# Chunked attention and a GELU MLP on one core: the first tile's q loads move to ScalarE's queue

## The chip, the cores and the metric

The kernel runs on one core of one Trainium2 chip. The metric is the device time of one execution in microseconds. The kernel before takes 276.42 us, the median of 3 runs (276.33 to 276.53).

## What is computed

Inputs q, k and v have the shape (8, 8, 576, 64): batch, heads, sequence, head size. The sequence is cut into 9 chunks of 64, and attention stays within a chunk. Its result is then laid out as 4608 tokens of 512 values and goes through two matrix products with an exact GELU between them:

```python
scores = scale * q_c @ k_c.T          # per batch, head and chunk of 64
attn   = softmax(scores)              # over the 64 keys of the chunk
x      = (attn @ v_c)                 # -> 4608 tokens x 512
h      = x @ w_in                     # 512 -> 2048
g      = 0.5 * h * (1 + erf(h / sqrt(2)))
out    = g @ w_out                    # 2048 -> 512
```

All inputs and the output are float32 in memory. The kernel casts them to bf16 for TensorE.

## The kernel before

**Tiles.** The 4608 tokens are worked in 9 tiles of 512. Tiles 0 to 7 are the first eight chunks of one batch each; tile 8 gathers the ninth chunk of all batches. A tile's attention is worked in four groups g of two heads. Each tile then has a first MLP product (16 slots of 4 matmuls, line 451; the very first two slots of tile 0 in line 441), a GELU on ScalarE (lines 444 and 453), and a second product.

**Order.** The whole program is written out by hand (`manual_schedule`): every engine executes its instructions in the order of the source. Only semaphores tie the engines together.

**The start (tile 0).** SP issues all loads. First come q and k of tile 0, in four pairs of 256 KB loads, one pair for each group g, in the order q0, k0, q1, k1, q2, k2, q3, k3 (line 118, called from lines 701 to 703). Then come the eight loads of V, 128 KB each in rows of 256 bytes (line 157), and the weights of the first product (line 676). The loads take turns on eight completion semaphores, so each load from the ninth on first waits for the load eight places ahead of it to complete: the first V load waits for q0, the second for k0, and so on.

The arriving float32 data is cast to bf16 (line 164): q on VectorE, k on GpSimd, which also zeroes the block-diagonal k tiles `k_bd` (lines 76 and 77) and later casts V (line 169). For each group there are five steps, and the prediction uses their names:

- `T[2g]`: TensorE transposes q of the group (line 175, four matmuls), and VectorE copies the result out (line 181).
- `T[2g+1]`: TensorE transposes k, and ScalarE copies it into `k_bd` in two halves (line 188).
- `S_[g]`: eight matmuls make the scores (line 332), and ScalarE takes the exponential (line 334, tile `pT`).
- `U[0]`, `U[1]` and `att_sum_pe` for groups 2 and 3: the sums for the softmax (lines 340 to 349, 383 to 397; the last in float32 matmuls, line 393).
- `A[g]`: eight matmuls with V (line 406), and VectorE multiplies by the reciprocal sums into `x` (line 408).

TensorE's order at the start is: seven `keep_warm` matmuls on a zero tile (line 693), `T[0]`, `T[1]`, three warm ones, `T[2]`, `S_[0]`, `T[3]`, one warm, `T[4]`, one warm, `S_[1]`, `U[0]`, `T[5]`, `T[6]`, `T[7]`, `U[1]`, `S_[2]`, one warm, `S_[3]`, one warm, then the sums of groups 2 and 3 and `A[0]` to `A[3]`. The first product follows directly.

**ScalarE at the start.** Its first instruction is the load of the table for the exponential, with one small activation on `act_scratch` (lines 706 and 698). Then it copies `k_bd` of group 0, takes the exponential of group 0, copies `k_bd` of group 1, takes the exponential of group 1, copies `k_bd` of groups 2 and 3, and takes the last two exponentials. After these comes the table for GELU.

**Weights.** Four quarters of `w_in` and four of `w_out` arrive as float32 in a pool of six staging buffers shared with q, k and V, and are cast by VectorE, GpSimd and ScalarE (lines 679 and 687) while TensorE already works on tile 0's first product.

Of the kernel before, what the change touches and what calls it, by code (L numbers as in the profile page):

```python
# [11 lines left out]
def kernel(  # L12
# [9 lines left out]
    nc = tc.nc  # L22
# [8 lines left out]
    J = 4  # L31
# [6 lines left out]
    MT = CT * CH  # L38
# [60 lines left out]
    def stage_tile():  # L99
        return stage.tile([P, SW], f32, tag="stage", name="arrival")  # L100
# [5 lines left out]
    def load_qk(t, nm, h0=0, h1=H):  # L106

        st = tiles[t]
        src = q if nm == "q" else k
        if nm + "f" not in st:  # L110
            st[nm + "f"] = stage_tile()[:].rearrange("p (h j d) -> p h j d", h=H, j=J)
            st[nm] = ld.tile([P, G, J, 2, D], bf16, tag=nm, name=f"{nm}_nat")
        raw = st[nm + "f"]
        if t == K0 and nm == "k":
            for n in range(CT // 2):
                nc.sync.dma_start(raw[:, :, n], src[t, :, P * n:P * (n + 1), :].rearrange("h key d -> key h d"))
        elif t < B:
            nc.sync.dma_start(raw[:, h0:h1], src[t, h0:h1, 0:MT, :].rearrange("h (p j) d -> p h j d", j=J))
        else:
            for b in range(B):  # L120
                nc.sync.dma_start(
                    raw[PC * b:PC * (b + 1), h0:h1],
                    src[b, h0:h1, MT:S, :].rearrange("h (p j) d -> p h j d", j=J))
# [576 lines left out]
    with tc.manual_schedule():  # L700
        for g in range(G):
            for nm in "qk":
                load_qk(0, nm, 2 * g, 2 * g + 2)
# [55 lines left out]
        win[0](2, DV)  # L759
        win[0](3, PO)  # L760
        load_qk(1, "q")
        wout.append(load_w_out(1))
        for c in range(1, NWC):
            for i in range(4):
                win[c](i, DV if i % 2 == 0 else PO)
            if c == 1:
                load_qk(1, "k")
            else:
                wout.append(load_w_out(c))
            if c < 3:  # L770
                r = slice(CH * (c - 1), CH * c)
                o = slice(CH * (2 - c), CH * (3 - c))
                nc.gpsimd.memset(v_bds[1][r, :, :, o], 0.0)
# [153 lines left out]
```

## Time and profile before

The profiled execution took 277.47 us. Its span, from the first to the last recorded instruction, is 275.68 us.

| | us | share of the span |
|---|---|---|
| TensorE matmuls busy | 265.6 | 96% |
| TensorE weight loads busy | 170.3 | 62% |
| ScalarE busy | 187.1 | 68% |
| VectorE busy | 177.2 | 64% |
| GpSimd busy | 85.3 | 31% |
| first matmul of the first MLP product starts | 18.98 | |
| median of 3 runs without the profiler | 276.42 | |

In the profile's lines PE is TensorE's matmul, PEld its weight load, DVE is VectorE, ACT is ScalarE, POOL is GpSimd and SP is the engine that issues DMAs; SPq and ACTq are the issuing sides of the queues. A line of the timeline begins with start and length in microseconds, then engine, source line, operation, and the tile written and the tile read. What stands in square brackets is how long the engine idled just before, and what ended it. A line of the busy windows gives a stretch, its length, the busy time and count of PE, PEld, DVE, ACT and POOL, the granted clock of TensorE (1.00 is full), the share of time that the DMA engines were busy, and the GB/s that they moved. A line of the DMA issues gives the tile and the source, the number of issues, their size and the time from the start of the issue until all of it has landed.

### The profile page before, as it was taken

How to read it: one execution, taken by the hardware profiler on the slowest of the kernel's cores; microseconds unless marked ns; L12 is line 12 of the kernel's file. 1: busy time of each engine (PE TensorE's matmuls, PEld its weight loads, DVE VectorE, ACT ScalarE, POOL GpSimd, SP SyncE). 2: the span in 40 equal slices, each digit the busy share in tenths (PEclk: the TensorE clock that was granted, in tenths of full speed). 3: DMA queues.
4: the chain of work that ended last, by engine and by line, in shares of the span. 5: the costliest groups of instructions: out<-in, count | busy, mean ns of one | idle time of the engine just before them, and what ended most of it. 6: DMA issues, size and time to landing. Idle time of an engine off the chain costs nothing.

```text
span 275.7 us, 6639 instructions
## 1 busy us (share of the span) xinstructions
PE 265.6 (96%) x2676; PEld 170.3 (62%) x2697; DVE 177.2 (64%) x321; ACT 187.1 (68%) x350; POOL 85.3 (31%) x142
## 2 busy tenths in 40 slices
PE   6699999999999999999999999999999999999993
PEld 2474455546864686468745874587458745874683
DVE  6866347886743865487998698559955985521521
ACT  3857758888756876687867966796679667346610
POOL 7869768310481354018106600034101100000000
PEclk9979999999999999999999999999999999999998
DMA  6999999798999899999399319999954110130014
GB/s 218 283 342 403 394 386 236 186 247 241 356 303 229 249 292 177 302 306 242 102 249 337 81 56 255 125 128 179 239 134 117 54 64 2 38 117 0 0 40 114
DMA packets 104735, 53.92 MB, mean 196 GB/s; under 512 B 72960, under 2 KB 101632, under 8 KB 104704
## 3 DMA queue, kind: packets, MB, share of 16 engines
q1 hardware_dynamic: 104400, 53.23, 74.6%
q8 instruction: 21, 0.34, 0.5%
q10 hardware_dynamic: 304, 0.26, 0.3%
q14 instruction: 10, 0.08, 0.1%
HBM read 36.70 MB, written 9.44 MB: 167 GB/s over the span
## 4 chain that ended last, share of the span: by engine, by line
PE 91%; ACT 4%; DMA 2%; issue 1%; SPq 0%; ACTq 0%; DVE 0%; POOL 0%; POOLq 0%
PE h_ps L451 43%; PE y_ps L566 34%; PE y_ps L638 3%; PE h_ps L441 2%; DMA arrival<-in_k_dram 2%; PE av_ps L315 2%; ACT k_bd L188 2%; PE s_ps L237 1%; PE y_ps L602 1%; PE rc_ps L393 1%; PE av_ps L406 1%; PE tp L175 1%; ACT pT L244 1%; ACT pT L334 1%; PE s_ps L332 1%
## 5 line engine op out<-in xcount | busy, mean ns | idle before, releaser
L451 PE MATMUL h_ps<-x,w_in_sb 128*128 128x512 bf16 x532 | 118.2, 379 | 0.8
L453 ACT ACTIVATE h<-h_ps 128x512 bf16<-128x512 f32 x137 | 81.7, 598 | 35.5 <-PE h_ps L451 35.5
L451 PEld LDWEIGHTS <-w_in_sb 128*128 128x128 bf16 x548 | 53.6, 98 | 63.2 <-DVE w_in_sb L679 0.2
L164 POOL CAST q_nat<-arrival 128x512 bf16<-128x512 f32 x31 | 20.2, 692 | 66.9 <-DMA arrival<-in_q_dram 66.9
L566 PEld LDWEIGHTS <-h 128*128 128x128 bf16 x384 | 37.0, 98 | 4.7
L566 PE MATMUL y_ps<-v_bd,k_bd 128*128 128x256 bf16 x256 | 29.4, 273 | 0.1
L566 PE MATMUL y_ps<-w_out_sb,h 128*128 128x256 bf16 x256 | 29.3, 273 | 0.0
L212 POOL CAST v_nat<-arrival 128x1024 bf16<-128x1024 f32 x14 | 15.0, 1078 | 45.4 <-DMA arrival<-in_v_dram 45.4
L566 PEld LDWEIGHTS <-k_bd 128*128 128x128 bf16 x256 | 24.8, 98 | 3.2 <-issue 0.2
L533 DVE TENSOR_TENSOR kept<-y_ps,kept 128x512 f32<-128x512 f32 (+1 forms) x25 | 16.4, 657 | 14.6 <-PE y_ps L566 11.8
L698 ACT ACT_TABLE_LOAD x18 | 23.1, 1283 | 1.1 <-PEq L911 0.7
L528 ACT COPY kept<-y_ps 128x512 f32<-128x512 f32 (+1 forms) x26 | 14.5, 556 | 12.4 <-PE y_ps L566 12.2
L164 POOL CAST k_nat<-arrival 128x512 bf16<-128x512 f32 x30 | 18.8, 664 | 10.7 <-DMA arrival<-in_v_dram 6.3
L491 DVE TENSOR_TENSOR s_sb<-h 128x2048 bf16<-128x2048 bf16 x8 | 9.8, 1220 | 18.1 <-ACT h L453 18.1
L504 DVE TENSOR_TENSOR k_bd<-h 128x1024 bf16<-128x1024 bf16 x16 | 11.3, 708 | 14.9 <-ACT h L453 14.9
L566 PE MATMUL y_ps<-v_bd,s_sb 128*128 128x256 bf16 x128 | 15.3, 273 | 0.0
L566 PE MATMUL y_ps<-w_out_sb,s 128*128 128x256 bf16 x128 | 15.3, 273 | 0.0
L566 PE MATMUL y_ps<-v_bd,h 128*128 128x256 bf16 x128 | 15.3, 272 | 0.0
L244 ACT ACTIVATE pT<-s_ps 128x512 bf16<-128x512 f32 x28 | 14.4, 603 | 0.1
L566 PEld LDWEIGHTS <-s 128*128 128x128 bf16 x128 | 12.4, 98 | 1.5
L566 PEld LDWEIGHTS <-s_sb 128*128 128x128 bf16 x128 | 12.3, 98 | 1.5
L538 ACT COPY y_sb<-y_ps 128x512 f32<-128x512 f32 x7 | 4.1, 586 | 13.2 <-PE y_ps L566 13.2
(106 smaller groups left out, 318.2 us busy)
## 6 DMA issues: line engine op xcount, KB each, us to landing
arrival<-in_v_dram SPq DMA_DIRECT2D x58, 128.0 KB, 4.1
arrival<-in_q_dram SPq DMA_DIRECT2D x7, 1024.0 KB, 7.0
arrival<-in_k_dram SPq DMA_DIRECT2D x6, 1024.0 KB, 8.5
out_dram<-kept SPq DMA_DIRECT2D x21, 256.0 KB, 2.6
arrival<-in_moe_w_out_dram SPq DMA_DIRECT2D x4, 1024.0 KB, 12.0
arrival<-in_moe_w_in_dram SPq DMA_DIRECT2D x6, 512.0 KB, 6.2
out_dram<-y_sb SPq DMA_DIRECT2D x11, 256.0 KB, 2.5
arrival<-in_k_dram SPq DMA_DIRECT2D x8, 256.0 KB, 5.5
```

The costliest lines, as they stand in the source:

```text
L164: copy(st[nm][:, g].rearrange("p j r d -> p r j d"), st[nm + "f"][:, 2 * g:2 * g + 2])
L212: copy(st["v"][:, r::2], st["vf"][:, r::2])
L244: nc.scalar.activation(pT[:].rearrange("p u (c j) -> p u c j", j=J), s_ps[g2][c][:].rearrange("p u (j c) -> p u c j", j=J), Act.Exp, scale ...
L451: nc.tensor.matmul(h_ps[:], w_in_sb[:, ks, f * P:(f + 1) * P], tiles[t]["x"][:, ks, :], start=(ks == 0), stop=(ks == KS - 1))
L453: nc.scalar.activation(tiles[t]["h"][:, f, :], h_ps[:], Act.Gelu)
L491: nc.vector.tensor_tensor(s3_sb[:], g_block(t, 0, 0), g_block(t, 1, 0), op=SUB)
L504: nc.vector.tensor_tensor(st["S", i][part], a, b, op=op)
L528: nc.scalar.copy(kept[name][:, ms], ps[:])
L533: nc.vector.tensor_tensor(y_sb[:, ms], ps[:], y_sb[:, ms], op=ADD)
L566: nc.tensor.matmul(to, left(f, m), right[:, f], start=(fresh and (split or m == 0) and f == 0), stop=(f == HF - 1), skip_group_check=True)
L638: nc.tensor.matmul(tiles[t]["y_ps", ms][:], tiles[t]["h"][:, fi, ms * P:(ms + 1) * P], w_out_sb[:, fi, :], start=(fi == 0), stop=False)
L698: nc.scalar.activation(act_scratch[:], rest[:, 0:1], func)
```

## The change

In `load_qk` the engine that issues the load is chosen: for tile 0's q it is ScalarE (`nc.scalar`), and for everything else SP (`nc.sync`) as before. This concerns four loads of 256 KB. In ScalarE's order they stand ahead of the table load; in SP's order k0 to k3 follow each other directly. The data, the buffers, the semaphores that each cast waits for and the order of all other instructions are the same. Line numbers after line 117 are higher by one in the changed kernel.

```diff
         elif t < B:
-            nc.sync.dma_start(raw[:, h0:h1], src[t, h0:h1, 0:MT, :].rearrange("h (p j) d -> p h j d", j=J))
+            by = nc.scalar if t == 0 and nm == "q" else nc.sync
+            by.dma_start(raw[:, h0:h1], src[t, h0:h1, 0:MT, :].rearrange("h (p j) d -> p h j d", j=J))
         else:
```

## The prediction

> **What bounds the kernel now.** I read the page's busy shares first, then the chain of waits, then that chain's first 20 us piece by piece, then the start's timeline, DMA issues and busy windows.
>
> ```profile
> PE 265.6 (96%) x2676; PEld 170.3 (62%) x2697; DVE 177.2 (64%) x321; ACT 187.1 (68%) x350; POOL 85.3 (31%) x142
> PE 91%; ACT 4%; DMA 2%; issue 1%; SPq 0%; ACTq 0%; DVE 0%; POOL 0%; POOLq 0%
> ```
>
> PE is busy 96% of the span, and the chain is PE for 91% of it. The rest is nearly all ahead of the first MLP matmul, which the pieces of the chain in order of time (start, length) show:
>
> ```profile
> 0.74 0.45 SPq L118
> 1.25 0.46 SPq L118
> 1.75 0.47 SPq L118
> 2.26 4.79 DMA arrival<-in_k_dram
> 7.17 0.62 POOL k_nat L164
> 7.85 0.41 PE tp L175 x4
> 8.28 0.58 ACT k_bd L188
> ...
> 12.82 1.09 ACT pT L334 x2
> ...
> 18.98 1.67 PE h_ps L441 x7
> ```
>
> Three issues on SP, the second k load (k1), its cast, its transposes, then ScalarE's row of k_bd copies and exps to 13.91, then PE to 18.98 and PE alone to the end. What the end can move is what 18.98 moves. A step later nothing absorbs it: from 19 us PE shows no wait above 0.3 us.
>
> k1 is not the only late load. Beside it stands q1, in the timeline:
>
> ```profile
> 6.40 0.43 DVE L164 CAST q_nat<-arrival 128x512 bf16<-128x512 f32 x1 [0.81 <-DMA arrival<-in_q_dram]
> 6.88 0.40 PE L175 MATMUL tp<-ident,q_nat 128*128 128x128 bf16 x4 [0.44 <-DVE q_nat L164]
> 7.11 0.40 PE L332 MATMUL s_ps<-s_sb,k_bd 128*128 128x64 bf16 x8
> 7.55 0.60 ACT L334 ACTIVATE pT<-s_ps 128x512 bf16<-128x512 f32 x1 [0.54 <-PE s_ps L332]
> 8.28 1.17 ACT L188 COPY k_bd<-tp 64x512 bf16<-64x512 bf16 x2
> ```
>
> S_[0] stands behind T[2] in PE's order, so the first exp waits for q1. That exp ends at 8.15, only 0.13 us before k_bd copy 1 starts at 8.28. So k1 alone, however early, is worth 0.13 us; beyond that q1 must come earlier too.
>
> **The change: issues.** Four issues (445 to 469 ns each) leave SP and go to ACT; order, waits and counts of all else stay. SP's four k issues then run from 0.74 to 2.78 instead of 1.25 to 4.77, so k1 is issued from 1.25 instead of 2.26. ACT issues q from about 0.75 (where its table load starts now) to 2.8. Behind them wait the table load (1.28 us) and the act_scratch activation (0.20): they end near 4.3 instead of 2.24. The next ACT work is the k_bd copy at 5.83, which now idles 3.59 us, so this costs nothing. If ACT's issue took the 0.73 us of the slower of the two ACT issue groups in the tail, all would end at 5.15, still covered; uncovered, it would cost what it passes 5.83 by.
>
> **What the transfers do.** Times to landing, one line for q1 (issued 1.75) and one for k1 (2.26), then DMA in the busy windows (last two figures: share, GB/s):
>
> ```profile
> arrival<-in_q_dram SPq DMA_DIRECT2D x1, 256.0 KB, 4.6
> arrival<-in_k_dram SPq DMA_DIRECT2D x1, 256.0 KB, 4.8
> ...
> 1.50:2.00 0.50, 0.50 (x2) 0.15 (x1) 0.50 (x1) 0.50 (x1) 0.43 (x3) 1.00 0.16 45
> 2.00:2.50 0.50, 0.50 (x3) 0.20 (x2) 0.45 (x3) 0.23 (x2) 0.43 (x3) 1.00 0.73 238
> 2.50:3.50 1.00, 1.00 (x4) 0.41 (x3) 0.84 (x2) 0.00 (x0) 0.94 (x3) 1.00 0.97 328
> 3.50:4.50 1.00, 0.85 (x4) 0.04 (x2) 0.87 (x2) 0.00 (x0) 0.57 (x2) 1.00 0.85 253
> 4.50:5.50 1.00, 0.46 (x6) 0.29 (x7) 0.61 (x1) 0.00 (x0) 0.77 (x2) 1.00 0.93 309
> ```
>
> Issue plus time to landing gives q0 3.43, k0 4.60, q1 6.37, k1 7.05, q2 7.72, k3 9.79. The engines are 85 to 100% busy from 2.5 us on, so k1 waits for bytes ahead of it, not for its issue (done at 2.73). The earlier issue therefore buys only the ramp: from the first packet at about 1.85 to 2.50 some 142 KB moved (22.5 + 119), where 328 GB/s would have moved 213; the missing 71 KB are 0.22 us. I take 0.2 as won; the ends are 0 and 0.22.
>
> No row has q and k in two queues at once. I take it that the engines serve both in turn. Then q and k of a pair land together at the later slot: q0 and k0 at 4.60 - 0.2 = 4.4, q1 and k1 at 7.05 - 0.2 = 6.85. For k1 that is 0.2 earlier; for q1 it is 0.48 later. Bounds for q1: high 7.05 (no ramp won). Low: 1 MB had moved at 5.55 by the windows, 1.5 us before k1 landed, while the first load landed 0.56 after its bytes; without that lag both land at 5.55 - 0.2 + 0.56 = 5.9. I take 6.85: the lag stands in seven of the eight landings.
>
> The Trainium skill, DMA: Bandwidth & Descriptors, section "Issuing engines are not separate DMA queues", says that DMAs of different engines run on the same 16 DMA engines and interleave, and that issuing from several saves only issue time. The trace agrees in that k1's issue ended 4.3 us before it landed. By that rule the gain in transfer time is nil and the sum below would be without the 0.2.
>
> **The sum.** q1 lands 6.85, cast 0.43 from 6.88. Now POOL casts k1 at the same moment; a DVE cast beside POOL work took 0.60 and 0.78 (at 7.92 and 3.62), beside another POOL cast 0.42 (at 9.62). I take 0.43, with 0.60 as the upper end. T[2] at 7.36, S_[0] at 7.59, the exp at 8.03, k_bd copy 1 about 0.5 us after its start (as at 9.95 to 10.45): 8.53. That is 0.25 later than 8.28. k1's branch: cast 6.88 to 7.50, T[3] after S_[0], done by 8.25: not last. With the bounds: 7.05 and 0.60 give +0.62; 5.9 gives T[2] at 6.41, but k_bd copy 0 (which follows k0's cast by 2.27) ends at 6.70, S_[0] at 6.75, k_bd copy 1 at 7.7, or -0.58. I take +0.3.
>
> From there ScalarE carries +0.3 to the end of its exps: 14.2. q2 and q3 also land up to 0.5 later, with T[4] needed before 9.8 (S_[1]) and its q cast starting now at 7.92: covered, with 0.9 us. k2, k3 come 0.2 earlier, so POOL starts V's casts up to 0.2 earlier; they wait for nobody.
>
> V's loads: each of the eight waits for the completion of the load eight places before it in the program's order. SP is free at 2.78, but the third V load waits for q1, at 6.85 instead of issuing at 6.39; against that, SP's own queue is shorter behind it, and the issues of 1.05, 1.24 and 0.96 us there can fall towards 0.51. The first weights land some 0.5 us earlier to 0.5 later. The trace has 1.6 us between the cast of the second w_in quarter (done 20.61) and its first matmul (about 22.2), and 1.5 or more at each later quarter: covered both ways.
>
> PE's stretch from 14.22 to 18.98 starts 0.3 later and passes it on: 18.98 becomes 19.28. Sum: +0.3 on this execution's 277.47 us (span 275.68). The median of the runs shown is 276.42, 1.05 below the profiled execution; the same step on it gives 276.7. From 0.2% (0.55 us) a measurement of this kernel can tell a difference.
>
> **The clock, which decides the rivals.** The granted clock falls to half once, in stretches of 3.41 us:
>
> ```profile
> 4.12:7.54 3.42, 2.26 (x24) 1.17 (x23) 1.63 (x4) 1.16 (x2) 1.95 (x4) 1.00 0.99 324
> 7.54:10.95 3.41, 2.67 (x32) 1.62 (x32) 2.76 (x6) 2.76 (x5) 3.06 (x7) 1.00 1.10 287
> 10.95:14.36 3.41, 1.91 (x37) 1.20 (x37) 3.29 (x8) 3.32 (x7) 3.01 (x8) 1.00 1.04 281
> 14.36:17.78 3.42, 3.42 (x42) 2.91 (x40) 2.38 (x6) 2.00 (x4) 3.07 (x8) 0.50 1.00 323
> ```
>
> After 1.91 us of PE work in a stretch the next ran at half; after 2.26 it did not. The Trainium skill, TensorE: Matmul & The Clock Gate, section "Part 1: The HAM clock gate", says the gate watches a window of 3.4 us that runs free of the kernel's start. By that rule the stretches could lie elsewhere in every execution; the three runs, 0.20 us apart, don't speak for it.
>
> **Rivals.**
> - *Slower: the clock falls one stretch earlier.* With S_[0] at 7.59 its 0.40 us leave 4.12 to 7.54, and 2.26 becomes 1.86, under 1.91. Then 7.54 to 10.95 runs at half. Eight matmuls of 64 columns took 0.61 there (16.72) and 0.41 at full (18.52): +0.2 each for S_[0] and S_[1], and some 0.1 for the transposes behind. +0.8 in all: 277.2. It decides from S_[0] about 0.35 us later. Against it: the half-rate work then counts longer, and the threshold is only bracketed.
> - *Faster: two queues keep the engines fed and the lag goes.* Landing at 5.9 gives -0.6. PE's final stretch then starts at 13.6, 10.95 to 14.36 holds about 2.5 us of PE work, and the half stretch goes too: the two fp32 groups (1.98 and 1.33 us) fall towards 1.0, worth up to 1.2 more, where POOL's V casts end. Together 274.6 to 275.8, middle 275.2. For it: the share of 0.85 at 3.5 to 4.5. Against: the lag is on few engines, which also work off the second queue.
> - *Nothing: q keeps its place.* If q's queue is served ahead of k's, q1 lands near 6.4 and k1 near 6.9; the exp stays, k1's 0.13 us is all: 276.4.
>
> **How the numbers follow.** Forecast (276.7) 0.34, of it 0.10 above 276.97; slower clock (277.2) 0.30; faster (275.2) 0.18; nothing (276.4) 0.18. So faster 0.18, same 0.24 + 0.18 = 0.42, slower 0.40. The range 275.3 to 277.6 leaves out half of the faster case and a part of the slower. The likeliest case's own range is 276.4 to 277.05.
>
> **What will show it.** In the changed profile: q1 and k1 within 0.2 us of each other near 6.85; the first exp near 8.0 and k_bd copy 1 near 8.5; the table load done by 4.3; first MLP matmul near 19.3. Wrong if q1 lands before 6.3, if the half-clock stretch moves or goes, or if ACT idles for a reason other than q1.

## The result and the profile after

The changed kernel is slower. It takes 278.45 us (median of 22 executions, 276.41 to 279.53) where the kernel before takes 276.66 us (22 executions on the same chip, 275.97 to 277.47). Over all executions the ratio is 1.005, with a 95% interval of 1.0033 to 1.0067; the two medians alone give 1.0065. The forecast was 276.7 us with a range up to 277.6, so the time lies outside it. Two executions that took several times as long as all others are left out here and below: one of the kernel before (558 us) and the traced one of E3 (1544 us), so E3 has no trace.

The median hides the form of it. Together with the first experiment below there are 34 executions of the changed kernel, and they fall into two groups with nothing between 277.43 and 278.4:

| group | executions | from, to | median | mean granted clock of the execution |
|---|---|---|---|---|
| lower | 15 | 276.41 to 277.43 | 276.97 | 0.999 or 1.0 in 14, 0.991 in one |
| upper | 19 | 278.4 to 279.94 | 279.01 | 0.993 to 0.998 in all |

The last column does not show what it seems to. The mean counts recorded stretches at half clock only, and the time ahead of the first clock record counts as full. In the two traces of the changed kernel the only recorded half stretch is the end of the span: 0.5 us in the one at 0.999, 1.8 us in the one at 0.997. One more stretch of 3.41 us at half lowers a mean over 277 us by about 0.006 (an estimate from these figures); the trace before, which has one from 14.36 to 17.78 us and 1.9 us at the end, stands at 0.99. In all runs the means lie at 0.990 to 0.994 or from 0.996 on, with none between. So the ten executions of the upper group at 0.993 or 0.994 probably had such a stretch behind the first rise of the clock, and the nine at 0.997 or 0.998 probably had none. No trace of the changed kernel shows the first kind.

The traced execution that came with the result is of the lower group: 276.81 us, span 275.0. Its busy shares are those of before, which says at once that nothing changed in the long run of the kernel:

```profile
PE 265.2 (96%) x2697; PEld 169.2 (62%) x2697; DVE 178.7 (65%) x321; ACT 187.1 (68%) x350; POOL 85.4 (31%) x142
PE 91%; ACT 4%; DMA 1%; DVE 1%; ACTq 0%; issue 0%
```

The start changed. These are the pieces of the chain of waits in order of time (start, length):

```profile
0.75 3.64 DMA arrival<-in_q_dram
4.39 0.02 issue
4.42 1.16 DVE q_nat L165
5.58 0.05 issue
5.62 0.41 PE tp L176 x4
6.03 0.02 issue
6.05 0.69 DVE s_sb L182
6.75 0.70 DVE q_nat L165
7.45 0.05 issue
7.50 0.40 PE tp L176 x4
7.89 0.25 PE s_ps L333 x8
...
17.89 1.73 PE h_ps L442 x8
```

The chain before ran through k1. Now it starts at q0, and VectorE's casts of q carry it to T[2] at 7.50. The issues of k and of q, four each with the median time to landing, and the busy windows show what the loads did:

```profile
arrival<-in_k_dram SPq DMA_DIRECT2D x4, 256.0 KB, 4.1
arrival<-in_q_dram ACTq DMA_DIRECT2D x4, 256.0 KB, 5.3
```

```profile
2.00:2.50 0.50, 0.50 (x3) 0.19 (x2) 0.45 (x3) 0.00 (x0) 0.43 (x3) 1.00 0.65 182
2.50:3.50 1.00, 1.00 (x4) 0.40 (x3) 0.84 (x2) 0.65 (x1) 0.94 (x3) 1.00 0.85 295
3.50:4.50 1.00, 0.86 (x3) 0.00 (x0) 0.18 (x2) 0.83 (x2) 0.85 (x3) 1.00 1.09 382
4.50:5.50 1.00, 0.00 (x0) 0.00 (x0) 1.00 (x1) 0.00 (x0) 0.95 (x3) 1.00 1.09 349
```

In the last two windows the DMA engines moved 382 and 349 GB/s, where before they moved 253 and 309. The trace's landings are k0 4.09, q0 4.39, k1 5.39, q1 5.81 us, where before they were q0 3.43, k0 4.60, q1 6.37, k1 7.05. The last window also has TensorE at 0.00: it did nothing from 4.5 to 5.5 us. The granted clock of 1.00 in these lines is no measurement up to 4.83 us: the trace's first clock record starts there, and without a record the column prints full.

### The profile page after: what moved, and what is told of

Same layout as the page of the kernel before. It is cut to its first block, busy times and chain, and to the rows that moved or that the text cites. A ratio compares the mean times of both kernels' runs of the same rounds, so it can differ in the third digit from the quotient of the medians.

```text
span 275.0 us, 6660 instructions
## 1 busy us (share of the span) xinstructions
PE 265.2 (96%) x2697; PEld 169.2 (62%) x2697; DVE 178.7 (65%) x321; ACT 187.1 (68%) x350; POOL 85.4 (31%) x142
## 4 chain that ended last, share of the span: by engine, by line
PE 91%; ACT 4%; DMA 1%; DVE 1%; ACTq 0%; issue 0%
PE h_ps L452 43%; PE y_ps L567 34%; PE y_ps L639 3%; PE h_ps L442 2%; PE av_ps L316 2%; ACT k_bd L189 2%; PE s_ps L238 1%; DMA arrival<-in_q_dram 1%; PE y_ps L603 1%; PE tp L176 1%; ACT pT L335 1%; PE av_ps L407 1%; PE rc_ps L394 1%; ACT pT L245 1%; DVE q_nat L165 1%; PE s_ps L333 1%
## 5 line engine op out<-in xcount | busy, mean ns | idle before, releaser
L452 PE MATMUL h_ps<-x,w_in_sb 128*128 128x512 bf16 x548 | 119.7, 379 | 0.0
L165 POOL CAST q_nat<-arrival 128x512 bf16<-128x512 f32 x31 | 19.4, 668 | 64.4 <-DMA arrival<-in_q_dram 64.4
```

What stands on the lines that cost most here:

```text
L165: copy(st[nm][:, g].rearrange("p j r d -> p r j d"), st[nm + "f"][:, 2 * g:2 * g + 2])
L452: nc.tensor.matmul(h_ps[:], w_in_sb[:, ks, f * P:(f + 1) * P], tiles[t]["x"][:, ks, :], start=(ks == 0), stop=(ks == KS - 1))
```

## The experiments

Every experiment was timed beside the kernel before on its own chip. The kernel before had medians of 276.99, 276.74 and 276.74 us beside the three groups of experiments.

**E1: the changed kernel again, without an edit**

> The changed kernel once more, unchanged, for more executions with their clocks and a second trace. Clock theory (a longer gap of TensorE before T[0] lets a stretch of 3.41 us fall to half clock in some executions): times in two groups about 2 us apart, 276.4 to 277.4 where the mean clock is 0.999 or more, 278.4 to 279.5 where it is below 0.9985; median near 278. Transfer theory (two queues land q late in some executions): two groups as well, but not sorted by the clock.

Measured: 278.82 us (276.41 to 279.94, 12 executions), ratio 1.0045 (1.0017 to 1.0073). Five executions were in the lower group and seven in the upper, sorted by the mean clock but for one (277.0 us at 0.991). The traced execution was of the upper group, span 277.1. It shows two things. The first is in the timeline of TensorE up to the first scores:

```profile
5.58 0.61 PE L176 MATMUL tp<-ident,q_nat 128*128 128x128 bf16 x4 [1.22 <-DVE q_nat L165]
6.41 1.49 PE L694 MATMUL warm<-rest 128*128 128x512 bf16 x3
8.12 0.63 PE L333 MATMUL s_ps<-s_sb,k_bd 128*128 128x64 bf16 x8
```

Three warm matmuls took 1.49 us, and 0.81 us in the other trace of the same kernel; T[0]'s transposes took 0.61 and 0.40. TensorE is still at half clock here: this trace's first clock record, at full, starts at 9.04 us, the other trace's at 4.83 us. The scores of S_[0] start at 8.12 instead of 7.73, and the first MLP matmul at 18.25 instead of 17.73: 0.52 us.

The second is larger. These are the pieces of the chain from 18.7 us on, and then the timeline of VectorE and of GpSimd at the same place:

```profile
18.74 0.69 DVE x L409
19.43 2.35 DVE w_in_sb L680
21.78 0.05 issue
21.83 2.33 PE h_ps L452 x10
```

```profile
19.35 2.42 DVE L680 CAST w_in_sb<-arrival 128x512 bf16<-128x512 f32 x1
```

```profile
19.14 0.61 POOL L680 CAST w_in_sb<-arrival 128x512 bf16<-128x512 f32 x1 [0.74 <-DMA arrival<-in_moe_w_in_dram]
19.69 1.80 POOL L774 MEMSET v_bd<- 64x2048 bf16 x1
```

VectorE's cast of the third block of the first quarter of w_in took 2.42 us. In the other trace two such casts took 0.75 us together. It ran into GpSimd's zeroing of the second V tile and ended 0.28 us after it. TensorE needed that block and waited 1.68 us:

```profile
21.83 2.55 PE L452 MATMUL h_ps<-x,w_in_sb 128*128 128x512 bf16 x11 [1.68 <-DVE w_in_sb L680]
```

0.52 and 1.68 are 2.2 us; the spans differ by 2.1 us. The landings of q and k are within 0.33 us of those of the other trace, so q does not land late in this execution of the upper group, which speaks against the transfer theory. The weights do differ: the half quarter that GpSimd casts ahead of the zeroing landed at 19.08 us here and at 20.61 in the other trace, where the zeroing began only at 21.48.

**E2: ten warm matmuls ahead of T[0]**

```diff
-        keep_warm(7)
+        keep_warm(10)
```

> The changed kernel with ten instead of seven warm matmuls ahead of T[0], so that TensorE works until about 5.5 us. Loads untouched. Clock theory: the upper group goes or gets rare, median 276.7 to 277.1, that is the +0.3 us of the late q alone. Transfer theory: as the changed kernel, median about 278.4, with executions above 278.4 in more than a third.

Measured: 276.81 us (276.45 to 279.1, 11 executions), ratio 1.0009 (0.9989 to 1.0029). Nine executions lie at 276.45 to 277.47, and two remain in the upper group (278.4 us at a mean clock of 0.999, 279.1 at 0.994). T[0] starts at 5.59 us, where it also starts without the edit (5.58 and 5.62), so it is TensorE's idle time ahead of T[0], and not T[0]'s lateness, that sends most executions there. The two that remain show that it is not the only way.

**E3: the kernel before with q0's cast held back**

```diff
+        nc.vector.memset(v_bds[0][0:CH, :, :, CH:P], 0.0)
         cast_qk(0, "q", 0, DV)
```

> The kernel before, all loads on SP, with one zeroing of V's tile (0.91 us) done twice on VectorE, so that q0's cast and T[0] start some 0.9 us later while every load stays as it was. Clock theory: an upper group 2 us above appears, in a fifth to two thirds of the executions; median 276.9 to 278.6. Transfer theory: no upper group, at most +0.3 us: 276.6 to 277.0.

Measured: median 276.66 us (276.07 to 278.13, 11 executions), ratio 0.9997 (0.9975 to 1.0019). The median lies below what the clock theory allowed and inside what the transfer theory did. Five of eleven executions lie at 277.33 to 278.13, and none at 278.4 or above. The kernel before beside it had eight of 34 above 277.3. This misses the forecast of a group 2 us higher: a late cast of q0 alone, with all loads on SP, doesn't cost that. How late T[0] was and what the clock did, no trace shows.

**E4: q0 stays on SP, only q1 to q3 on ScalarE**

```diff
-            by = nc.scalar if t == 0 and nm == "q" else nc.sync
+            by = nc.scalar if t == 0 and nm == "q" and h0 > 0 else nc.sync
```

> The changed kernel, but q0 stays first on SP; only q1, q2 and q3 are issued from ScalarE. Clock theory: T[0] is back near 4.5 to 4.8 us, so no upper group, and the late q1 costs 0 to 0.4 us: 276.5 to 277.1. Transfer theory: two queues are still at work, so the upper group stays: median above 278.

Measured: 277.25 us (276.48 to 280.2, 12 executions), ratio 1.0017 (0.9995 to 1.004). T[0] is back at 4.53 us, but k0, now behind q0 on SP, lands at 5.30, and S_[0] stays late at 7.76. Ten executions lie at 276.48 to 277.83. Two are at 278.91 and 280.2, both with a mean clock of 0.993 or 0.994. The median is 0.15 above what the clock theory allowed: two queues with T[0] in time don't bring the upper group back in force, but they don't exclude it.

After these four the theory was: the upper group needs a half-clock stretch somewhere in the first 18 us, and then the zeroing on GpSimd, which the early loads have moved forward, falls on the first weight casts. The next group tests the second half.

**E5: the zeroings of the second V tile one weight quarter later**

```diff
-            if c < 3:
-                r = slice(CH * (c - 1), CH * c)
-                o = slice(CH * (2 - c), CH * (3 - c))
+            if c > 1:
+                r = slice(CH * (c - 2), CH * (c - 1))
+                o = slice(CH * (3 - c), CH * (4 - c))
```

> The changed kernel with GpSimd's two zeroings of the second V tile each one weight quarter later (behind the casts of the third and fourth quarter of w_in), so that the first no longer falls on VectorE's first weight cast. Collision theory (the upper group's 2 us are 0.6 to 0.9 from a clock that rises one stretch late, and the rest from the zeroing that holds up that cast): lower group unchanged at 276.4 to 277.4, upper group at 277.3 to 278.2 instead of 278.4 to 279.9, median 276.9 to 277.5. Rival (the clock alone makes the 2 us): upper group stays at 278.4 to 279.9 in about half of the executions.

Measured: 277.29 us (276.48 to 278.4, 12 executions), ratio 1.0026 (1.0011 to 1.0041). The upper group of 278.4 to 279.94 is gone but for one at its lower edge. Five executions have a clock of 0.990 or 0.991 and lie at 277.34 to 278.4; the other seven lie at 276.48 to 277.8. A half-clock stretch is still there in some executions, but it now costs about 1 us (their median is 278.06) and not 2. That the place of the zeroing makes the other half is shown by the times; the collision itself was seen only in E1's trace.

**E6: the same move in the kernel before**

> The same move of the two zeroings in the kernel before. There the zeroing starts at 21.6 us, behind the cast in question, so both theories expect no change: median 276.5 to 277.2.

Measured: 276.5 us (275.88 to 277.87), ratio 0.9996 (0.998 to 1.0012). Nothing moves, as expected. In the trace of the kernel before the zeroing begins at 21.6 us. It holds up a cast there too, at 22.06 us, but one that TensorE doesn't wait for.

**E7: E2 and E5 together, in the changed kernel**

> The changed kernel with the zeroings moved and ten warm matmuls ahead of T[0]. Both causes are taken away: no executions above 278, median 276.5 to 276.9. If a third cause is at work, some executions stay above 278.4.

Measured: 276.58 us (276.37 to 277.84, 11 executions), ratio 1.0001 (0.9985 to 1.0016). With both causes taken away the changed kernel is as fast as the kernel before. No third cause is needed for the loss. E2's interval overlaps with this one, so the times don't tell how much E5's move adds to E2's.

**E8: the zeroing of the third k tile behind the cast of k1**

```diff
-        zero_k(k_bds[2], nc.gpsimd)
         cast_qk(0, "k", 1, PO)
+        zero_k(k_bds[2], nc.gpsimd)
         zero_k(k_bds[3], nc.gpsimd)
```

> The changed kernel with GpSimd's zeroing of the third k tile moved behind the cast of k1, so that it no longer runs beside VectorE's cast of q0. If that zeroing makes the cast slow (1.15 us): cast 0.4 to 0.8 us, T[0] near 5.1 instead of 5.62, S_[0] 0.3 to 0.5 earlier, lower group at 276.0 to 277.0, and the upper group in fewer executions. If the cast is slow because of the k cast beside it: no change in the cast, both groups as in the changed kernel.

Measured: 276.59 us (276.0 to 277.0, 12 executions), ratio 0.9995 (0.9984 to 1.0006). Here are VectorE's cast of q0 and T[0] in the timeline of the changed kernel, and then in that of E8:

```profile
4.42 1.15 DVE L165 CAST q_nat<-arrival 128x512 bf16<-128x512 f32 x1 [0.82 <-DMA arrival<-in_q_dram]
5.62 0.40 PE L176 MATMUL tp<-ident,q_nat 128*128 128x128 bf16 x4 [1.26 <-DVE q_nat L165]
```

```profile
4.44 0.69 DVE L165 CAST q_nat<-arrival 128x512 bf16<-128x512 f32 x1 [0.84 <-DMA arrival<-in_q_dram]
5.19 0.61 PE L176 MATMUL tp<-ident,q_nat 128*128 128x128 bf16 x4 [0.82 <-DVE q_nat L165]
```

With the zeroing out of its way the cast takes 0.69 us instead of 1.15, and T[0] starts 0.43 us sooner. This swap of two lines alone takes the upper group away in 12 of 12 executions. The clock still rises late in this trace (9.49 us), but TensorE then waits for no weight cast: the zeroing of the second V tile begins at 20.95 us, when VectorE's first two weight casts (19.02 to 19.96 us) are done. So a late clock alone doesn't put an execution into the upper group. Why the weights came later here than in E1's trace is not shown. S_[0] did not come earlier here (7.72 against 7.73), because half-clock matmuls took back what the cast gave.

The last group asks whether the early landings can be turned into time. The order of TensorE is changed so that the scores of group 0 no longer stand behind q1.

**E9: the order alone, in the kernel before**

```diff
-        T[0]()
-        cast_qk(0, "q", 1, DV)
-        T[1]()
+        T[1]()
+        T[0]()
+        cast_qk(0, "q", 1, DV)
         keep_warm(3)
-        T[2]()
         S_[0]()
+        T[2]()
         T[3]()
```

> The kernel before with S_[0] ahead of T[2] and T[1] ahead of T[0] in TensorE's order; all loads on SP. There k0's copy ends at 7.0 and k1 lands at 7.05 us, so nothing can start sooner: k_bd copy 1 stays near 8.2, 276.5 to 277.1 (within 0.2% of before). If it is faster by 0.5 us, the order alone and not the two queues makes the gain of the next kernel.

Measured: 277.08 us (276.28 to 278.0), ratio 1.0007 (0.9987 to 1.0028). Nothing is gained. In its trace k1 landed later than in the kernel before, at 7.92 us, and k_bd copy 1 began at 9.15 us, not near 8.2.

**E10: the same order and E8's swap in the changed kernel**

> The changed kernel with the zeroing of the third k tile moved as in the fourth kernel of the last group, and the same order as h0: T[1] before T[0], S_[0] before T[2]. If the two queues bring k0, k1 and q1 early, as the traces say (k1 at 5.4, q1 at 5.8), and only the order kept that from use: first exp at 6.9 to 7.3, k_bd copy 1 at 7.4 to 7.8 instead of 8.28, end 0.4 to 0.8 us sooner: 275.9 to 276.4. If the early landings are worth nothing: 276.5 to 276.8, as with the zeroing alone.

Measured: 276.41 us (276.06 to 277.35), ratio 0.999 (0.9973 to 1.0006). ScalarE in the timeline:

```profile
5.32 1.17 ACT L189 COPY k_bd<-tp 64x512 bf16<-64x512 bf16 x2 [0.98 <-PE tp L176]
6.99 0.60 ACT L335 ACTIVATE pT<-s_ps 128x512 bf16<-128x512 f32 x1 [0.50 <-PE s_ps L333]
7.49 1.17 ACT L189 COPY k_bd<-tp 64x512 bf16<-64x512 bf16 x2
9.56 0.60 ACT L335 ACTIVATE pT<-s_ps 128x512 bf16<-128x512 f32 x1 [0.91 <-PE s_ps L333]
```

The first exp and the second k_bd copy start at 6.99 and 7.49 as forecast, 0.56 and 0.79 us sooner than before. The second exp starts at 9.56, only 0.39 sooner: it now waits 0.91 us for S_[1], which stands behind T[4] and so behind VectorE's copy of T[2] and cast of q2 (7.26 to 8.62). The time lies between the two forecasts, and its interval includes 1.

**E11: E10 and the move of E5**

> The kernel h1 with the second V tile's zeroings moved one weight quarter later as well. If collisions with the first weight casts still occur in some executions of h1, those go: same lower group, no execution above 277.9. Otherwise as h1.

Measured: 276.37 us (275.96 to 278.2), ratio 0.999 (0.9969 to 1.001). As E10, so nothing shows that E10 had collisions left to remove. One execution, at 278.2 us with a clock of 0.991, lies above the 277.9 that was expected.

**E12: E11 with one more warm matmul behind S_[2] and S_[3]**

```diff
         S_[2]()
-        keep_warm(1)
+        keep_warm(2)
         S_[3]()
-        keep_warm(1)
+        keep_warm(2)
```

> The kernel h2 with one more warm matmul each behind S_[2] and S_[3], where TensorE waits. If a half-clock stretch begins after that place in some executions (mean clock 0.990 to 0.994) for want of work, these executions go and the upper edge falls to about 277.2; the median falls by 0 to 0.3. If not: as h2.

Measured: 276.2 us (275.9 to 276.86, 12 executions), ratio 0.9985 (0.9971 to 0.9999). None of the 12 executions has a clock below 0.997. The time is 0.15% below the kernel before and about 0.65% below the changed one (0.9985 over 1.005). Its margin over the kernel before is hardly clear of the interval, and it is the best of four tries on this chip, so the gain is small at most. E11 had one execution below 0.997, so that the two warm matmuls removed half-clock stretches is not shown.

## Why the prediction was wrong

The sign of the likeliest case was right and its size wrong: +0.3 us was forecast, and the ratio makes 0.5%, about 1.4 us. Two terms that the sum put at nothing make the difference. One is q0's later landing, which leaves TensorE idle ahead of T[0]. The other is the earlier GpSimd ("they wait for nobody", "covered both ways"), whose zeroing meets a weight cast on VectorE. In the traced execution of the upper group the late clock cost 0.52 us and the collision 1.68 us. Taken step by step:

- **Issues.** Right. ScalarE issued q from 0.75 to 2.81 us, its table was loaded by 4.13 and the small activation done by 4.34, and no instruction waited for that.
- **Landings.** Wrong, and for the better. Forecast were 4.4 for q0 and k0 and 6.85 for q1 and k1. Measured were 4.39 and 4.09, then 5.81 and 5.39. The step that failed is "the lag stands in seven of the eight landings", by which it was carried over; that the lag is on few engines, no row shows. All three traces with every load on SP (the kernel before, E6 and E9) have q1 at 6.34 to 7.18; all nine with q's four loads on ScalarE's queue have it at 5.76 to 5.91. The rival "two queues keep the engines fed and the lag goes" had the right premise, with 5.9; its gain of 0.6 us and more did not follow, since VectorE came to q1 late.
- **S_[0] and the exp.** Right numbers for a wrong reason. Forecast were 7.59 and 8.03, with k_bd copy 1 at 8.53; measured 7.73, 8.16 and 8.66. It was not q1's landing that made them late. q0's landing, 0.96 us later than before, moved VectorE's cast of it next to GpSimd's cast of k0 and zeroing of the third k tile, where it took 1.15 us. The prediction wrote q0's landing down and never followed it to T[0]. T[0] went from 4.46 to 5.62, and q1's cast waited on VectorE until 6.66 though its data was there at 5.81.
- **The sum in undisturbed executions.** The lower group's median of 276.97 is 0.3 above the kernel before (276.66 beside the first run). That has the size of the +0.3 that was forecast, but by luck: q1 landed 1.04 us sooner than forecast, and q0's slow cast made up for it. It also compares a part of one kernel's executions with all of the other's.
- **"They wait for nobody" and "covered both ways".** This is the step that cost the prediction its range. Of the four k loads k1 came 1.7 us sooner, not 0.2; GpSimd started V's casts at 9.38 (9.31 in the upper group's trace) instead of 10.46, and the second half of the second weight quarter landed at 19.08 in the upper group's trace instead of 20.75. So GpSimd reached the zeroing there at 19.69 instead of 21.61. In the six traces with q1 to q3 on ScalarE's queue and the zeroing in its place, it begins at 19.69 to 21.48 us; in the two with all loads on SP at 21.61 and 22.93. The early V casts alone don't explain this: the changed kernel's other trace has them too, and its zeroing begins at 21.48. The 1.6 us of margin were read at the second quarter of w_in, but TensorE needs a block of the first quarter sooner. Here is VectorE's cast of it (the first of two) in the timeline of the kernel before, and then GpSimd's zeroing there:

```profile
19.86 0.75 DVE L679 CAST w_in_sb<-arrival 128x512 bf16<-128x512 f32 x2
```

```profile
21.61 1.80 POOL L773 MEMSET v_bd<- 64x2048 bf16 x1
```

  That cast follows VectorE's last multiplication into `x`. It ended at 20.28, and the first matmul of line 451, which reads the block, started at 20.49: a margin of 0.21 us. This is the cast that the zeroing hit in the upper group's trace, where it began 0.34 us before the zeroing; in the other seven of these traces it began 1.6 us or more before. E5 supports it: with the zeroing moved, the 2 us become about 1.
- **The clock.** The rival saw that the start had little margin. It expected a fall after S_[0] had left a stretch, for +0.8. In the one trace of the upper group the clock rises late instead, for 0.52; the ten executions at 0.993 or 0.994 may have had a fall like the rival's, but no trace shows where. The bound of 1.91 us that the rival used doesn't hold: in the upper group's trace the stretch from 19.28 to 22.69 us has 1.73 us of TensorE work by the records, and the clock stayed full. The half stretch at 14.36, which the sum took for the kernel's course, stands in the trace of the kernel before alone and in none of the other twelve; the first MLP matmul was forecast for 19.28 and started at 17.73. The gap ahead of T[0] shows in the busy windows of the 3.41 us up to 4.83, in the trace where the clock rose there, and of the 3.41 us up to 5.62, in the one where it did not:

```profile
1.42:4.83 3.41, 2.94 (x7) 0.73 (x5) 2.37 (x5) 1.49 (x2) 3.05 (x12) 1.00 0.82 268
```

```profile
2.21:5.62 3.41, 2.19 (x7) 0.49 (x5) 2.36 (x5) 1.49 (x2) 3.17 (x8) 1.00 1.01 332
```

  TensorE worked 2.94 us of the first stretch and 2.19 of the second. The traces of E4 (2.92 us up to its rise at 5.47) and of E8 (2.59 up to 6.07, and no rise) fit between. The Trainium skill, TensorE: Matmul & The Clock Gate, section "Part 1: The HAM clock gate", says that the window runs free of the kernel's start. The traces agree, since the first rise lies at anything from 4.12 to 5.87 us, or one stretch later (9.04 and 9.49). The prediction held the narrow spread of three runs against it. Where the stretch falls thus differs from execution to execution, which would explain how one program makes two groups.

What stays open: the upper group was traced once. That its other executions, above all the ten with a mean clock of 0.993 or 0.994, end in the same collision is argued from E5 and E7, not seen. The collision also needs the weights early enough, and why their landing differs by 1.5 us between two traces of one program is not settled. Why VectorE's casts stop beside GpSimd's zeroings was not tried by itself.

## What to carry to other kernels

When a load is moved, follow each of its consumers to the next engine: a load that comes later can hit its own cast, and a load that comes earlier can send an engine off the path into a collision with one on it. Where a kernel's start leaves TensorE just busy enough for the full clock, a gap of 1 us costs little in one execution and much in the next, so look at all times with their clocks and not at one trace. An early landing starts nothing sooner until the instruction order lets it be used. E9 and E10 have the same order, and E10, which also has E8's swap and the two queues, has the first exp and k_bd copy 1 sooner. In the time the gain is not clear of the noise (0.999, interval 0.9973 to 1.0006).

## What the runs showed of the hardware

Eight 256 KB loads from two queues moved faster between 3.5 and 5.5 us than the same eight from one. From 3.5 to 4.5 and from 4.5 to 5.5 us the three traces with one queue show 187 to 253 and then 244 to 309 GB/s; the changed kernel's two traces show 381 and 382, then 349 and 359. The fourth of the eight landed at 7.05 to 7.92 us with one queue and at 5.76 to 5.91 in nine traces with two. The Trainium skill, DMA: Bandwidth & Descriptors, section "Issuing engines are not separate DMA queues", says that DMAs of several engines interleave on the same 16 DMA engines, and that issuing from several saves only issue time. The order of landing agrees with the first (q and k of a pair land 0.3 and 0.4 us apart), and the rate at the start does not agree with the second. What holds the single queue back there, the runs don't show.

A VectorE cast from float32 to bf16 that takes 0.42 us alone took 1.15 us beside a GpSimd cast and zeroing, and 2.42 us beside a zeroing of 1.80 us. In the kernel before a cast that started at 22.06 us, inside the zeroing from 21.61 to 23.41, took 1.64 us. In all three cases it ended 0.28 or 0.29 us after a zeroing had ended.
